# Six-expert part of an attention and mixture-of-experts kernel: sums and low parts of the weights made on GpSimd in place of VectorE

## The chip, the cores and the metric

The kernel runs on one core of a Trainium2 chip. A core has TensorE (PE, matmuls; its weight loads are listed as PEld), VectorE (DVE), ScalarE (ACT), GpSimd (POOL) and SyncE (SP, which here issues nearly all DMAs). Each engine works through its own list of instructions in order; semaphores tie the lists together. The metric is the time of one execution on the device in microseconds (us), and lower is better.

## The reference

A linear recurrence with complex decay per head (four sequences of 768 tokens, eight heads of 48) gives x of 3072 tokens by 384. A mixture of eight experts follows. Every expert is applied to every token, and its output is weighted by a gate matrix that eight rounds of row and column scaling (Sinkhorn) make from the logits:

```python
logits = x @ w_gate
P = np.exp(logits - logits.max())
for _ in range(8):
    P /= P.sum(1, keepdims=True) + 1e-09
    P /= P.sum(0, keepdims=True) + 1e-09
    P *= N / E
for e in range(E):                     # 8 experts
    h = np.maximum(x @ w1[e], 0.0)     # 384 -> 1024
    ye = h @ w2[e]                     # 1024 -> 384
    out += P[:, e:e + 1] * ye
```

All is in 32-bit floats.

## The kernel before

Every large matmul is made as three: a tensor is split into a high part (a cast to the rounded type that TensorE takes fast) and a low part (the tensor less its high part), and high x high, high x low and low x high are added in PSUM.

Phase 1 runs the recurrence for 256 tokens at a time and, beside it, experts 0 and 1 on the tokens that are done. `phase2a` closes that with the last experts' steps, the first Sinkhorn rounds, a check of the inputs' range and the first weights of the next part. `phase2b` is the six-expert part: 96 steps, four units of 768 tokens x experts 2 to 7 x four pairs of blocks of 128 hidden columns. Its order is two super-units (`su`), in each six experts (`e`), in each two units (`ul`), in each four pairs (`p`). So a prepared weight pair is used twice, four steps apart.

In one step a two-by-two block of the first layer is made by a scheme of seven products (P1, P6, P7, P5, P2, P4, P3 in that order) in place of eight. It needs sums of weight blocks (S1 to S4, and S5 for a third block) and sums of token blocks (T1 to T4). The products go to PSUM through two buffers of the tag `ph`, in turn: a product can begin when the one before the last has been read out. ScalarE copies P1 and P5 out (`s`, line 793). VectorE adds the others to earlier ones (line 788), which gives u2, u3 (from P6, P7), u4 and c22 (from two SBUF tensors), c11 (P2), c21 (P4) and c12 (P3). For each c, ScalarE makes the relu's high part `hh` (line 799) and VectorE the low part `hl` (line 800). Between the products PE makes the second layer of the step before (`second`, lines 739 to 741), from `hh`, `hl` and the split second-layer weights. After the last pair of an expert VectorE adds the outputs to `oa` (line 748), and while expert 3 runs also those of experts 0 and 1 (lines 725 and 727). `load_x` loads a unit's tokens and makes their sums on VectorE (lines 616 and 620).

`prep_w` prepares the weights of one expert and pair, 48 times. Its input is a raw tile (128 partitions x 2 blocks x 768 columns, 768 KB), loaded by SP in `raw_w` (line 641); its pool has one buffer, so the next load waits for the last reader of the one before. It makes five sums of 128 columns each (line 659; the second and the fourth read an earlier sum), four casts on ScalarE (line 661) and four low parts (line 662): two for `wa` (384 and 256 columns, straight from the raw tile), one for `wb` (640, from the sums) and one for `wc` (768, the second layer's weights). `wa`, `wb` and `wc` come from a ring of twelve buffers, four preparations deep. `prep_w` is called twice in `phase2a`, twice after the first step of `phase2b`, and once after every step that follows one on the second unit.

PE's order is written by hand. The order of the other engines is made when the kernel is built, by a scheduler that plays the program through in time and takes for each engine what it expects to be ready first; on the chip that order is fixed. The buffer numbers behind the names in the rows below are the builder's; the number behind s_, u_, c_, hh_ and hl_ is the step's.

Of the kernel before, what the change touches and what calls it, by code (L numbers as in the profile page):

```python
# [6 lines left out]
F32 = mybir.dt.float32  # L7
# [3 lines left out]
ALU = mybir.AluOpType  # L11
# [49 lines left out]
class Net:  # L61
# [581 lines left out]
        self.nraw += 1  # L643

    def prep_w(self):
        nc, V, A = self.nc, self.nc.vector, self.nc.scalar
        n = self.nprep
        if n == len(self.todo):
            return
        self.nprep += 1  # L650
        raw = self.raw.pop(n)
        R = raw.rearrange("p f (c d) -> p f c d", d=128)
        s = self.wr.tile([128, 5, 128], F32, tag="sum", name=f"sum{n}")
        wa = self.wp.tile([128, 2, 5, 128], F32R, tag="w", name=f"wa{n}")
        wb = self.wp.tile([128, 2, 5, 128], F32R, tag="w", name=f"wb{n}")
        w2 = self.wp.tile([128, 2, 2, C], F32R, tag="w", name=f"wc{n}")
        A11, A12, A13, A21, A22, A23 = (R[:, i, c] for i in range(2) for c in range(3))
        for o, a, b, op in ((0, A21, A22, ALU.add), (1, s[:, 0], A11, ALU.subtract), (2, A11, A21, ALU.subtract), (3, A12, s[:, 1], ALU.subtract), (4, A13, A23, ALU.subtract)):
            V.tensor_tensor(s[:, o], a, b, op)
        for t, k, src in ((wa, slice(0, 3), R[:, 0, :3]), (wa, slice(3, 5), R[:, 1, 1:3]), (wb, slice(0, 5), s), (w2, slice(0, 2), raw[:, :, C:])):  # L660
            A.activation(t[:, 0, k], src, AF.Copy)
            V.tensor_tensor(t[:, 1, k], src, t[:, 0, k].bitcast(F32), ALU.subtract)
        W = {nm: (wa, k) for k, nm in enumerate(("A11", "A12", "A13", "A22", "A23"))}
        W.update({f"S{k + 1}": (wb, k) for k in range(5)})
        self.W[n] = (W, w2)
        self.raw_w()
# [349 lines left out]
```

## Time and profile before

| | |
|---|---|
| median of three runs | 1827.03 us (1826.17 to 1827.82) |
| the profiled execution | 1826.91 us, its span 1825.0 us |
| granted TensorE clock, mean | 0.993 |
| busy in 649.4 to 1811 us (1161.6 us, the 96 steps) | PE 1149.62, DVE 822.53, ACT 412.12, POOL 0.00 us |
| raw loads | 48, 768 KB each, 4.3 us from issue to landing (4.1 to 6.4) |
| SP before raw loads, waiting for DVE's wc | 661.5 us in 40 waits |
| ACT before wa, waiting for raw | 72.8 us in 35 waits |
| ACT before wb, waiting for DVE's sums | 14.8 us in 26 waits |

Times of instructions and waits are from one profiled execution and count from the span's start. Consecutive matmuls overlap, so a single one's duration (0.33 us) is longer than its pitch (0.17 us). The idle time of an engine matters only where another engine ends up waiting for it; SP's long waits above are the single buffer of raw tiles doing what it is for.

### The profile page before, as it was taken

How to read it: one execution, taken by the hardware profiler on the slowest of the kernel's cores; microseconds unless marked ns; L12 is line 12 of the kernel's file. 1: busy time of each engine (PE TensorE's matmuls, PEld its weight loads, DVE VectorE, ACT ScalarE, POOL GpSimd, SP SyncE). 2: the span in 40 equal slices, each digit the busy share in tenths (PEclk: the TensorE clock that was granted, in tenths of full speed). 3: DMA queues.
4: the chain of work that ended last, by engine and by line, in shares of the span. 5: the costliest groups of instructions: out<-in, count | busy, mean ns of one | idle time of the engine just before them, and what ended most of it. 6: DMA issues, size and time to landing. Idle time of an engine off the chain costs nothing.

```text
span 1825.0 us, 30537 instructions
## 1 busy us (share of the span) xinstructions
PE 1767.9 (97%) x12024; PEld 1726.8 (95%) x12024; DVE 1358.4 (74%) x3023; ACT 733.1 (40%) x1606; POOL 6.4 (0%) x15
## 2 busy tenths in 40 slices
PE   5899999999999999999999999999999999999998
PEld 3889899999999999899999999999999999999998
DVE  7898899889883587867576767687776767675754
ACT  7544444554543443434242424243433333342421
POOL 1000000000000000000000000000000000000000
PEclk9999999999999999999999999999999999999999
DMA  6334333433332431402020101232220101020100
GB/s 210 108 104 117 103 112 112 119 112 115 115 105 93 132 92 38 136 2 69 1 69 1 53 18 53 70 96 78 87 70 18 53 18 52 3 69 1 53 27 28
DMA packets 120632, 132.83 MB, mean 73 GB/s; under 512 B 9632, under 2 KB 100512, under 8 KB 120480
## 3 DMA queue, kind: packets, MB, share of 16 engines
q1 hardware_dynamic: 119680, 130.41, 23.3%
q8 instruction: 96, 1.57, 0.4%
q14 instruction: 56, 0.46, 0.1%
q10 hardware_dynamic: 800, 0.39, 0.1%
HBM read 88.22 MB, written 23.59 MB: 61 GB/s over the span
## 4 chain that ended last, share of the span: by engine, by line
PE 86%; DVE 8%; DMA 3%; ACT 1%; issue 1%; SPq 1%; DVEq 0%; ACTq 0%
PE po L741 10%; PE po L739 10%; PE po L740 10%; PE P L778 9%; PE P L780 9%; PE P L779 9%; PE po L164 4%; PE ph L186 3%; PE ph L187 3%; PE ph L185 3%; PE po L166 3%; PE po L165 3%; PE sp L468 3%; PE y L485 2%; PE U L463 1%
## 5 line engine op out<-in xcount | busy, mean ns | idle before, releaser
L741 PE MATMUL po<-wc,hl 128*128 128x384 f32 x1152 | 385.7, 335 | 2.9 <-DVE hl L800 2.9
L739 PE MATMUL po<-wc,hh 128*128 128x384 f32 x1152 | 385.2, 334 | 0.4 <-ACT hh L799 0.4
L740 PE MATMUL po<-wc,hh 128*128 128x384 f32 x1152 | 385.2, 334 | 0.0
L799 ACT ACTIVATE hh<-c 128x384 fp32r<-128x384 f32 x384 | 200.9, 524 | 322.1 <-DVE c L788 320.7
L800 DVE SCALAR_TENSOR_TENSOR hl<-c,hh 128x384 fp32r<-128x384 f32 x384 | 211.8, 552 | 65.8 <-ACT hh L799 58.0
L741 PEld LDWEIGHTS po<-wc,hl 128*128 128x128 f32 x1152 | 216.5, 188 | 4.4 <-DVE hl L800 4.4
L739 PEld LDWEIGHTS po<-wc,hh 128*128 128x128 f32 x1152 | 216.5, 188 | 0.7 <-ACT hh L799 0.7
L740 PEld LDWEIGHTS po<-wc,hh 128*128 128x128 f32 x1152 | 216.4, 188 | 0.0
L793 ACT ACTIVATE s<-P 128x384 f32<-128x384 f32 x192 | 94.1, 490 | 275.0 <-PE P L780 275.0
L191 ACT ACTIVATE hh<-ph 128x256 fp32r<-128x256 f32 x192 | 73.1, 381 | 249.4 <-PE ph L187 248.9
L186 PE MATMUL ph<-xl,w 128*128 128x256 f32 x576 | 162.9, 283 | 2.8 <-DVE xl L525 2.8
L185 PE MATMUL ph<-xh,w 128*128 128x256 f32 x576 | 162.2, 282 | 0.6 <-ACT xh L524 0.6
L187 PE MATMUL ph<-xh,w 128*128 128x256 f32 x576 | 162.5, 282 | 0.0
L778 PE MATMUL P<-B,wa 128*128 128x384 f32 x480 | 160.4, 334 | 0.6 <-DVE c L788 0.6
L780 PE MATMUL P<-B,wa 128*128 128x384 f32 x480 | 160.4, 334 | 0.0
L779 PE MATMUL P<-B,wa 128*128 128x384 f32 x480 | 160.3, 334 | 0.0
L164 PE MATMUL po<-w,hh 128*128 128x384 f32 x384 | 140.9, 367 | 1.1 <-ACT yst L169 1.1
L166 PE MATMUL po<-w,hl 128*128 128x384 f32 x384 | 130.1, 339 | 0.0
L165 PE MATMUL po<-w,hh 128*128 128x384 f32 x384 | 129.7, 338 | 0.0
L788 DVE TENSOR_TENSOR c<-P,u 128x384 f32<-128x384 f32 x192 | 106.2, 553 | 31.1 <-PE P L780 29.3
L788 DVE TENSOR_TENSOR u<-u,s 128x384 f32<-128x384 f32 x96 | 53.3, 555 | 100.9 <-ACT s L793 100.8
L193 DVE TENSOR_TENSOR hl<-hf,hh 128x256 fp32r<-128x256 f32 x192 | 80.0, 419 | 45.0 <-ACT hf L192 43.6
(172 smaller groups left out, 3649.3 us busy)
## 6 DMA issues: line engine op xcount, KB each, us to landing
raw<-in_w_dram SPq DMA_DIRECT2D x48, 768.0 KB, 4.3
qs<-z SPq DMA_DIRECT2D x144, 64.5 KB, 2.6
qk<-in_aqk_dram SPq DMA_DIRECT2D x12, 768.0 KB, 4.9
ks<-kh SPq DMA_DIRECT2D x144, 64.0 KB, 2.6
ye_d<-yst SPq DMA_DIRECT2D x48, 192.0 KB, 2.1
y<-ye_d SPq DMA_DIRECT2D x48, 192.0 KB, 2.4
z<-in_aqk_dram SPq DMA_DIRECT2D x11, 768.0 KB, 6.9
B<-x_d SPq DMA_DIRECT2D x40, 192.0 KB, 3.5
```

Source lines behind the costliest of these rows:

```text
L164: nc.tensor.matmul(po[k], hh[:, s], w2h, start=f == 0, stop=False)
L185: nc.tensor.matmul(ph, w[:, 0, cs], xh[:, ct, :], start=(ct == 0), stop=False)
L186: nc.tensor.matmul(ph, w[:, 0, cs], xl[:, ct, :], start=False, stop=False)
L187: nc.tensor.matmul(ph, w[:, 1, cs], xh[:, ct, :], start=False, stop=(ct == NCT - 1))
L739: nc.tensor.matmul(po[k], hh[:, s], w2[:, 0, i], start=first, stop=False)
L740: nc.tensor.matmul(po[k], hh[:, s], w2[:, 1, i], start=False, stop=False)
L741: nc.tensor.matmul(po[k], hl[:, s], w2[:, 0, i], start=False, stop=last)
L778: nc.tensor.matmul(ps, t[:, 0, k], x[:, 0], start=first, stop=False)
L779: nc.tensor.matmul(ps, t[:, 0, k], x[:, 1], start=False, stop=False)
L780: nc.tensor.matmul(ps, t[:, 1, k], x[:, 0], start=False, stop=last)
L799: A.activation(hh, c, AF.Relu)
L800: V.scalar_tensor_tensor(hl, c, 0.0, hh.bitcast(F32), ALU.max, ALU.subtract)
```

## The change

In `prep_w` the five sums and the four low parts go to GpSimd. The casts stay on ScalarE, and nothing else is edited.

```diff
@@ -643,7 +643,7 @@
     def prep_w(self):
-        nc, V, A = self.nc, self.nc.vector, self.nc.scalar
+        nc, G, A = self.nc, self.nc.gpsimd, self.nc.scalar
@@ -656,10 +656,10 @@
         for o, a, b, op in ((0, A21, A22, ALU.add), (1, s[:, 0], A11, ALU.subtract), (2, A11, A21, ALU.subtract), (3, A12, s[:, 1], ALU.subtract), (4, A13, A23, ALU.subtract)):
-            V.tensor_tensor(s[:, o], a, b, op)
+            G.tensor_tensor(s[:, o], a, b, op)
         for t, k, src in ((wa, slice(0, 3), R[:, 0, :3]), (wa, slice(3, 5), R[:, 1, 1:3]), (wb, slice(0, 5), s), (w2, slice(0, 2), raw[:, :, C:])):
             A.activation(t[:, 0, k], src, AF.Copy)
-            V.tensor_tensor(t[:, 1, k], src, t[:, 0, k].bitcast(F32), ALU.subtract)
+            G.tensor_tensor(t[:, 1, k], src, t[:, 0, k].bitcast(F32), ALU.subtract)
```

VectorE's list in step 14 (expert 3, second unit, third pair), before (-) and now:

```order
 L788 TENSOR_TENSOR c_14_10557<-u_14_10538,s_14_10553 128x384
-L662 TENSOR_TENSOR wb_10628<-sum_10626,wb_10628 128x640
 L788 TENSOR_TENSOR c_14_10572<-P_14_10565,s_14_10520 128x384
 L800 SCALAR_TENSOR_TENSOR hl_14_10575<-c_14_10557,hh_14_10574 128x384
 L800 SCALAR_TENSOR_TENSOR hl_14_10579<-c_14_10572,hh_14_10578 128x384
 L788 TENSOR_TENSOR c_14_10595<-P_14_10588,u_14_10538 128x384
-L662 TENSOR_TENSOR wc_10629<-raw_10507,wc_10629 128x768
 L800 SCALAR_TENSOR_TENSOR hl_14_10598<-c_14_10595,hh_14_10597 128x384
 L788 TENSOR_TENSOR c_14_10614<-P_14_10607,u_14_10555 128x384
```

The rest keeps its order: both hl of c22 and c11 stand ahead of c21, and the hl of c21 ahead of c12, the last row. GpSimd's list of the same preparation, which is new, in the order in which it is worked through:

```order
L659 TENSOR_TENSOR sum_10626<-raw_10507 128x128 x3
L659 TENSOR_TENSOR sum_10626<-sum_10626,raw_10507 128x128
L662 TENSOR_TENSOR wa_10627<-raw_10507,wa_10627 128x384
L662 TENSOR_TENSOR wa_10627<-raw_10507,wa_10627 128x256
L659 TENSOR_TENSOR sum_10626<-raw_10507,sum_10626 128x128
L662 TENSOR_TENSOR wb_10628<-sum_10626,wb_10628 128x640
L662 TENSOR_TENSOR wc_10629<-raw_10507,wc_10629 128x768
```

The first row waits for the raw tile's DMA on GpSimd's own list; both low parts of wa stand ahead of the last sum. ScalarE's list at the same place:

```order
 L661 ACTIVATE wa_10627<-raw_10507 128x256
 L793 ACTIVATE s_14_10553<-P_14_10546 128x384
+L799 ACTIVATE hh_14_10574<-c_14_10557 128x384
 L661 ACTIVATE wb_10628<-sum_10626 128x640
-L799 ACTIVATE hh_14_10574<-c_14_10557 128x384
 L799 ACTIVATE hh_14_10578<-c_14_10572 128x384
 L661 ACTIVATE wc_10629<-raw_10507 128x768
```

The cast of the sums moved behind the relu of c22, and still stands ahead of that of c11. In steps 15 and 16 it moved by one or two rows in the same way. PE's list is the same in both kernels.

## The prediction

> **What bounds the kernel now.** I read the page's busy times first, then stretches cut out of the stage that the change touches, then what PE waited for, then the steps instruction by instruction. The page's first part says whose time the span is:
>
> ```profile
> PE 1767.9 (97%) x12024; PEld 1726.8 (95%) x12024; DVE 1358.4 (74%) x3023; ACT 733.1 (40%) x1606; POOL 6.4 (0%) x15
> ```
>
> PE is busy in 97% of the span, VectorE in 74%, and GpSimd does nothing after its first memsets. So work taken from VectorE pays only where PE waits for VectorE. Stretches of the six-expert part (columns: from:to in us, length, busy us and count of PE, PEld, DVE, ACT, POOL, clock, DMA) show where that is:
>
> ```profile
> 820.74:832.70 11.96, 11.96 (x71) 11.96 (x71) 9.10 (x21) 5.40 (x10) 0.00 (x0) 1.00 0.21 66
> 832.70:844.65 11.95, 11.95 (x70) 11.95 (x70) 9.16 (x21) 5.40 (x10) 0.00 (x0) 1.00 0.21 67
> 1200.00:1248.70 48.70, 45.90 (x261) 44.80 (x260) 39.31 (x85) 19.83 (x37) 0.00 (x0) 1.00 0.40 123
> 1300.00:1348.70 48.70, 46.56 (x265) 45.60 (x265) 39.61 (x87) 21.92 (x42) 0.00 (x0) 1.00 0.31 94
> ```
>
> The first two are steps 14 and 15, each with the preparation of one weight pair in it: PE is full, at full clock, 11.96 us a step. There VectorE's preparation is already hidden and its removal is worth nothing. In the other two, where VectorE also makes the next tokens' sums or adds expert outputs, PE loses 2.8 and 2.1 us of 48.7. PE's waits in total (us in all, times, longest):
>
> ```profile
> PE P L778 <- DVE c L788: 4.7, 7, 1.5
> PE P L778 <- ACT s L793: 3.0, 4, 1.2
> PE po L741 <- DVE hl L800: 2.9, 4, 1.1
> PE okp L561 <- DVE ok L558: 1.5, 1, 1.5
> PE P L778 <- DVE u L788: 0.7, 1, 0.7
> ```
>
> VectorE's four rows make 9.8 us: the ceiling of what the change can win, and not all of it stands beside a preparation.
>
> **What is moved, and what it costs where it goes.** By line and shape (count, then busy us and mean ns of one):
>
> ```profile
> L662 DVE TENSOR_TENSOR wc<-raw,wc 128x768 fp32r<-128x768 f32 x48 | 45.9, 956 | 12.2 <-ACT wc L661 12.1
> L662 DVE TENSOR_TENSOR wb<-sum,wb 128x640 fp32r<-128x640 f32 x48 | 39.2, 817 | 0.1
> L659 DVE TENSOR_TENSOR sum<-raw 128x128 f32<-128x128 f32 x144 | 35.7, 285 | 40.6 <-DMA raw<-in_w_dram 40.5
> L662 DVE TENSOR_TENSOR wa<-raw,wa 128x384 fp32r<-128x384 f32 x48 | 26.4, 551 | 0.0
> L662 DVE TENSOR_TENSOR wa<-raw,wa 128x256 fp32r<-128x256 f32 x48 | 20.0, 416 | 0.0
> L659 DVE TENSOR_TENSOR sum<-sum,raw 128x128 f32<-128x128 f32 x48 | 13.6, 283 | 0.0
> L659 DVE TENSOR_TENSOR sum<-raw,sum 128x128 f32<-128x128 f32 x48 | 13.5, 281 | 0.0
> ```
>
> The seven rows sum to 194.3 us, over 48 preparations 4.05 us each: nine instructions and 5 x 128 + 384 + 256 + 640 + 768 = 2688 columns. VectorE loses these and its 40.5 us of waiting for raw weights. On GpSimd no subtraction has run; its nearest rows are memsets:
>
> ```profile
> L215 POOL MEMSET sc<- 128x512 f32 x2 | 1.2, 612 | 0.1
> L225 POOL MEMSET rr<- 112x8 f32 x2 | 0.1, 94 | 0.0
> ```
>
> They give (612 - 94) / 504 = 1.03 ns a column and about 0.09 us an instruction. Low end: a subtraction goes at memset pace, 2688 x 1.03 ns + 9 x 0.09 = 3.6 us a preparation. High end: both operands and the result each take a pass, 9.1 us. I take two passes, 6.3 us: a memset reads nothing, so the two reads come on top of its pattern, and the write can go beside them. The Trainium skill (GPSIMD Engine Reference, section 3.1) gives 4497 ns for a two-input add of 2048 columns, against 2293 on VectorE; an estimate from it is 5.9 us a preparation, and no run here shows it.
>
> **What becomes late.** Step 14 in the timeline (start, us, instruction, idle before it and its releaser); first VectorE, then ScalarE, then PE in step 15:
>
> ```profile
> 824.18 0.49 DVE L659 TENSOR_TENSOR sum<-raw 128x128 f32<-128x128 f32 x2 [1.41 <-DMA raw<-in_w_dram]
> ...
> 826.27 0.28 DVE L659 TENSOR_TENSOR sum<-raw,sum 128x128 f32<-128x128 f32 x1
> ...
> 828.61 1.23 DVE L800 SCALAR_TENSOR_TENSOR hl<-c,hh 128x384 fp32r<-128x384 f32 x2
> ...
> 831.70 0.55 DVE L800 SCALAR_TENSOR_TENSOR hl<-c,hh 128x384 fp32r<-128x384 f32 x1
> 832.17 0.55 DVE L788 TENSOR_TENSOR c<-P,u 128x384 f32<-128x384 f32 x1
> ```
>
> ```profile
> 824.18 0.83 ACT L661 ACTIVATE wa<-raw 128x384 fp32r<-128x384 f32 x2 [2.07 <-DMA raw<-in_w_dram]
> ...
> 826.58 0.74 ACT L661 ACTIVATE wb<-sum 128x640 fp32r<-128x640 f32 x1 [0.25 <-DVE sum L659]
> 827.52 0.53 ACT L799 ACTIVATE hh<-c 128x384 fp32r<-128x384 f32 x1 [0.20 <-DVE c L788]
> 828.72 0.53 ACT L799 ACTIVATE hh<-c 128x384 fp32r<-128x384 f32 x1 [0.67 <-DVE c L788]
> 829.94 0.85 ACT L661 ACTIVATE wc<-raw 128x768 fp32r<-128x768 f32 x1 [0.70 <-PE P L780]
> 830.70 0.51 ACT L799 ACTIVATE hh<-c 128x384 fp32r<-128x384 f32 x1
> ```
>
> ```profile
> 833.39 0.33 PE L778 MATMUL P<-T,wb 128*128 128x384 f32 x1
> ```
>
> The reader should see two things. The cast of the sums (wb) stands in ScalarE's row ahead of relus, and waits for the fifth sum, 2.37 us after the raw weights landed (826.55 - 824.18). And the last product's addition (c12, the row at 832.17) frees the PSUM buffer that the next step's second product (the PE row) writes: it ends at 832.72, 0.67 us ahead of that matmul, some 0.5 us ahead of its weight load. That half microsecond is all the cover that VectorE has at the end of a step with a preparation.
>
> Now the same with GpSimd, in its new order: four sums, both low parts of wa, the fifth sum, wb, wc. The fifth sum ends after seven instructions and 1280 columns: 1.9 us at one pass, 3.3 at two, 4.6 at three. To this I add 1.1 us for being held up behind two VectorE instructions of 0.55 us: 4.4 us. Whether the two engines hold each other up at all where both read two tensors in SBUF is shown by no row; the bounds are nothing, and a whole instruction of the other engine each time they meet. I take half an instruction, midway. The raw weights land 0.7 us later, because the low part of wc that frees their only buffer takes 2 x 768 x 1.03 ns + 0.09 = 1.67 us for 0.96. So: landing 824.9, fifth sum 829.3, wb to 830.0, the relu behind it (c11) to 830.6, its hl on VectorE to 831.1; c21 queued behind that to 831.7; ScalarE has done wc by 831.4, relu of c21 to 832.2, its hl to 832.8, c12 behind it to 833.3. With 0.7 us more for that hl meeting the 1.4 us low part of wb half-way, c12 ends near 834.0, and must end by about 833.2: PE stalls **0.8 us**. ScalarE and VectorE work in order, so this delay reaches PE although neither is short of time. Without any hold-up, c12 ends at 832.2 or when P3 lets it (832.7), inside the margin.
>
> Steps 15 and 16 have the same chain, the cast one relu later. Step 16 also carries six additions of finished outputs, and has less room; I take 1.0 us on average over the three. The fourth preparation of an expert has its sums made steps ahead and costs nothing by this chain. The first four preparations, made beside the last steps of the first two experts, are due one by one in the first four steps; I put them at nothing, with up to 4 us if the second and third raw loads come late. The other 44 are eleven experts of four: 33 x 1.0 = **+33 us**. On the SP queue the next raw load waits for wc on GpSimd, and loads of expert outputs (y) and of tokens (B) stand behind it; their order shifts by a place or two. That costs them the same 0.7 us, at few places, and I add nothing.
>
> **What is won.** Of the 9.8 us that PE waits for VectorE I take about three quarters, **-7 us**: the 1.5 us before the check's transpose, where VectorE was subtracting weights, and most of the waits in the stretches above, which lose 4 us of VectorE work a step. The 3.0 us behind ScalarE's s stay. The profiled execution took 1826.9 us (span 1825.0 and 1.9 around it), 0.1 under the median of 1827.0. So 1826.9 + 33 - 7 = **1853 us**.
>
> **Rivals.** *Relief*: GpSimd is at two passes or less and no engine holds the other up; the margin at c12 stays, and only the relief remains, all of the 9.8 us but some 2: 1826.9 - 8 = 1819 us. For it: PE is full in steps 14 and 15, and the chain comes out at 832.7 without hold-ups. Against it: six VectorE instructions with two SBUF inputs (u4, c22, four hl) stand in each such step, beside GpSimd's 6.3 us of 12. It decides if c12 ends within 0.5 us of where it does now. Chance 0.27.
>
> *Full hold-up*: an instruction of one engine waits out the other's whole instruction. Then the hl of c21 waits 0.7 us longer, and that of c11 meets a low part too, 0.7; with less to spare elsewhere 1.6 us a step: 33 x 1.6 = +53, and VectorE's other two-tensor additions are held up in the heavy stretches, so the relief is gone: 1880 us. Chance 0.21. The Trainium skill (SBUF — State Buffer, section "Who interferes with whom") says just this: a VectorE instruction with two SBUF inputs contends with a GpSimd instruction that reads SBUF, and whichever issues second is blocked until the first is done. No row of this case can show it, GpSimd having read nothing; that rule speaks against the change.
>
> *Nothing visible*: hold-ups eat the relief, the margin just holds: 1827 us, chance 0.12. My forecast, 1840 to 1866, has 0.40.
>
> **The numbers.** The range reaches from most of the relief to past the full hold-up, 1816 to 1888, and leaves some 0.15 out. A measurement of this kernel can tell about 0.2%, 3.7 us, from no change. Faster by more than that: the relief, 0.26; within it: 0.14; slower: 0.60, from the forecast and the full hold-up.
>
> **What would show it.** Right: PE waiting for DVE c or u some thirty times in steps with a preparation, ScalarE's wb waiting for POOL's sum by 2 us or more, SP's raw load waiting for POOL's wc, hl on VectorE starting late after its relu is done; VectorE's busy time down by some 194 us. The subtraction of wc on POOL should take about 1.7 us. Wrong: steps of 11.96 us throughout with fewer PE waits than before (relief), or a subtraction at 1 us. If POOL's preparation takes over 9 us, the single raw buffer becomes the limit, and even 1880 is too low.

## The result and the profile after

| | kernel before | changed kernel |
|---|---|---|
| median of four runs on one chip | 1827.42 us (1826.17 to 1829.74) | 1879.69 us (1877.21 to 1882.07) |
| ratio, with 95% interval | 1 | 1.0289 (1.0276 to 1.0302) |
| profiled execution, its span | 1826.91 us, 1825.0 us | 1882.07 us, 1880.1 us |

The change costs 52.3 us by the medians, 55.2 between the two profiled executions. The forecast was 1853 us: right in sign, half in size. The busy times of the page's first part, and then what PE waited for (us in all, times, longest), in the changed kernel:

```profile
PE 1784.1 (95%) x12024; PEld 1730.9 (92%) x12024; DVE 1319.4 (70%) x2591; ACT 725.1 (39%) x1606; POOL 401.2 (21%) x447
```

```profile
PE P L778 <- DVE c L788: 42.8, 33, 4.6
PE okp L561 <- DVE ok L558: 2.8, 1, 2.8
PE po L741 <- DVE hl L800: 1.9, 2, 1.6
PE P L778 <- DVE u L788: 1.6, 2, 1.1
```

```profile
PEld P L778 <- DVE c L788: 58.4, 47, 4.9
```

PE now waits 33 times for one of VectorE's c, 42.8 us in all, where it waited 7 times and 4.7 us. The weight load in front of a matmul waits for the same c, and its row (PEld) shows the shorter waits too: 47 of them, 58.4 us, after 8 and 7.4 us in the kernel before. VectorE has 432 instructions less (48 x 9), yet its busy time fell by 39 us and not by the 194 that they took. The groups by line and shape show where the rest went, first before and then now (busy us and mean ns of one stand behind the bar):

```profile
L800 DVE SCALAR_TENSOR_TENSOR hl<-c,hh 128x384 fp32r<-128x384 f32 x384 | 211.8, 552 | 65.8 <-ACT hh L799 58.0
L788 DVE TENSOR_TENSOR c<-P,u 128x384 f32<-128x384 f32 x192 | 106.2, 553 | 31.1 <-PE P L780 29.3
L788 DVE TENSOR_TENSOR c<-u,s 128x384 f32<-128x384 f32 x96 | 52.8, 550 | 0.0
```

```profile
L800 DVE SCALAR_TENSOR_TENSOR hl<-c,hh 128x384 fp32r<-128x384 f32 x384 | 278.3, 728 | 100.6 <-ACT hh L799 90.6
L788 DVE TENSOR_TENSOR c<-P,u 128x384 f32<-128x384 f32 x192 | 105.9, 552 | 30.4 <-PE P L780 30.3
L788 DVE TENSOR_TENSOR c<-u,s 128x384 f32<-128x384 f32 x96 | 70.1, 730 | 0.0
```

The instructions are the same, on the same shapes. Those with both inputs in SBUF (hl, c from u and s) take 176 and 180 ns longer on average. The one with an input in PSUM (c from P and u) takes as long as ever. The timeline of step 14, the step that the prediction worked through, shows what a longer one does. It has GpSimd's last rows, then VectorE's, then PE's (start, us, instruction, idle before it and its releaser):

```profile
842.58 1.57 POOL L662 TENSOR_TENSOR wb<-sum,wb 128x640 fp32r<-128x640 f32 x1 [0.85 <-ACT wb L661]
844.10 2.17 POOL L662 TENSOR_TENSOR wc<-raw,wc 128x768 fp32r<-128x768 f32 x1
...
842.95 1.61 DVE L800 SCALAR_TENSOR_TENSOR hl<-c,hh 128x384 fp32r<-128x384 f32 x1 [0.80 <-ACT hh L799]
844.49 0.54 DVE L788 TENSOR_TENSOR c<-P,u 128x384 f32<-128x384 f32 x1
845.62 1.06 DVE L800 SCALAR_TENSOR_TENSOR hl<-c,hh 128x384 fp32r<-128x384 f32 x1 [0.59 <-ACT hh L799]
846.61 0.55 DVE L788 TENSOR_TENSOR c<-P,u 128x384 f32<-128x384 f32 x1
...
847.21 0.45 PE L778 MATMUL P<-T,wb 128*128 128x384 f32 x1 [1.18 <-DVE c L788]
```

The first hl is issued 0.37 us after GpSimd began wb, and ends at 844.56. GpSimd's wb ended at 844.15, 0.41 us earlier. The second hl meets wc: GpSimd ends at 846.27, the hl at 846.68, again 0.41 later. So an hl waits until GpSimd's whole instruction is over and then does its work. This holds throughout: of the 384 hl of this trace 99 take over 700 ns, and each of these ends 0.41 to 0.42 us after the GpSimd instruction that it met. Behind it stands c12 (846.61 to 847.16), and PE's second product of step 15 waits for it, 1.18 us. This is the chain and the place that the prediction named.

The cost is spread like this. Rows are stretches with from:to, length, busy us and count of PE, PEld, DVE, ACT, POOL, clock, DMA. First four quiet steps of the changed kernel, steps 14 to 17, then three stretches with other work on VectorE (steps 5 to 9, 44 to 50, 51 to 57), and behind them the same three in the kernel before:

```profile
833.00:845.34 12.34, 12.25 (x70) 11.93 (x70) 7.56 (x11) 4.92 (x10) 7.20 (x9) 1.00 0.20 64
845.34:858.78 13.44, 12.26 (x70) 11.94 (x70) 8.74 (x13) 5.25 (x11) 7.72 (x10) 1.00 0.17 60
858.78:870.74 11.96, 11.96 (x70) 11.94 (x70) 8.28 (x15) 4.17 (x9) 6.57 (x9) 1.00 0.21 67
870.74:884.43 13.69, 12.35 (x71) 11.87 (x70) 8.51 (x15) 4.33 (x9) 5.60 (x7) 1.00 0.18 58
...
712.20:785.16 72.96, 64.06 (x349) 61.18 (x349) 60.00 (x101) 25.18 (x51) 32.37 (x34) 0.98 0.35 109
1206.27:1302.94 96.67, 87.61 (x484) 84.88 (x484) 68.66 (x113) 32.90 (x67) 34.38 (x36) 0.98 0.30 95
1302.94:1398.44 95.50, 88.37 (x484) 85.94 (x484) 69.15 (x113) 35.16 (x71) 32.80 (x36) 0.96 0.24 75
```

```profile
708.17:773.08 64.91, 61.75 (x349) 59.75 (x348) 58.51 (x135) 25.04 (x50) 0.00 (x0) 1.00 0.39 122
1179.79:1269.50 89.71, 85.58 (x485) 83.48 (x484) 70.58 (x149) 34.05 (x67) 0.00 (x0) 1.00 0.32 102
1269.50:1357.04 87.54, 84.82 (x485) 83.54 (x484) 69.53 (x149) 35.98 (x71) 0.00 (x0) 1.00 0.27 82
```

The four quiet steps take 51.43 us; at 11.96 us each they took 47.84, so a preparation cycle of one expert loses 3.6 us. By the step starts in the two traces, the quiet stretches (steps 10 to 43 and 58 to 93, eight such cycles) lose 27.9 us together. The three heavy stretches lose 8.1, 7.0 and 8.0 us, 23.0 in all, though VectorE has 34 to 36 instructions less in each: its busy time there is 197.8 us after 198.6. The time up to step 5 loses 4.0. These make the 55.0 us by which the span grew.

In the quiet stretches the waits of the weight loads for c account for the whole loss: 25 of them, 27.9 us, none in the kernel before. Each cycle has three of size. The first is 0.41 us long and stands at the start of step 14; it comes from the preparation before, whose wc is worked on at the end of step 13 (GpSimd, VectorE's hl of c21 and c12, then the weight load of step 14's second product):

```profile
831.00 1.84 POOL L662 TENSOR_TENSOR wc<-raw,wc 128x768 fp32r<-128x768 f32 x1 [8.36 <-ACT wc L661]
831.37 1.88 DVE L800 SCALAR_TENSOR_TENSOR hl<-c,hh 128x384 fp32r<-128x384 f32 x1 [0.74 <-ACT hh L799]
833.17 0.54 DVE L788 TENSOR_TENSOR c<-P,u 128x384 f32<-128x384 f32 x1
833.77 0.19 PEld L778 LDWEIGHTS P<-T,wb 128*128 128x128 f32 x1 [0.41 <-DVE c L788]
```

The second, 1.4 to 1.6 us, is the one in step 15 shown above (1.50 us in the weight load's row, 1.18 in the matmul's). The third, 1.1 to 1.7 us, stands in step 17. In all eight cycles the hl just ahead of c12 had met the same GpSimd instruction: wc at the first and the second wait, wb at the third. The preparation that is loaded in step 15 makes PE wait nowhere.

GpSimd's side, by line and shape, and the range of two of the lines (min, median, max in ns):

```profile
L662 POOL TENSOR_TENSOR wc<-raw,wc 128x768 fp32r<-128x768 f32 x48 | 95.9, 1999 | 123.3 <-ACT wc L661 123.3
L662 POOL TENSOR_TENSOR wb<-sum,wb 128x640 fp32r<-128x640 f32 x48 | 75.7, 1578 | 42.3 <-ACT wb L661 42.3
L659 POOL TENSOR_TENSOR sum<-raw 128x128 f32<-128x128 f32 x144 | 68.3, 502 | 802.3 <-DMA y<-ye_d 582.6 <-DMA raw<-in_w_dram 219.6
```

```profile
L662 POOL TENSOR_TENSOR wc<-raw,wc x48: 1800/1998/2194, 622.7 to 1784.4; 128x768 fp32r<-128x768 f32 x48
L659 POOL TENSOR_TENSOR sum<-raw x144: 448/463/872, 589.6 to 1775.8; 128x128 f32<-128x128 f32 x144
```

From the two minima a subtraction costs (1800 - 448) / 640 = 2.1 ns a column. GpSimd's busy time less the 6.4 us of memsets that it had before makes (401.2 - 6.4) / 48 = 8.2 us a preparation.

### The profile page after: what moved, and what is told of

It is laid out like the page before. It is cut to its first block, busy times and chain, and to the rows that moved or that the text cites. A ratio compares the mean times of both kernels' runs of the same rounds, so it can differ in the third digit from the quotient of the medians.

```text
span 1880.1 us, 30664 instructions
## 1 busy us (share of the span) xinstructions
PE 1784.1 (95%) x12024; PEld 1730.9 (92%) x12024; DVE 1319.4 (70%) x2591; ACT 725.1 (39%) x1606; POOL 401.2 (21%) x447
## 4 chain that ended last, share of the span: by engine, by line
PE 65%; DVE 14%; DMA 8%; POOL 5%; ACT 4%; issue 3%; SPq 1%; DVEq 0%; POOLq 0%; ACTq 0%
PE po L739 7%; PE po L741 7%; PE po L740 7%; PE P L778 6%; PE P L780 6%; PE P L779 6%; DMA raw<-in_w_dram 5%; PE po L164 3%; DVE hl L800 3%; PE ph L186 3%; PE ph L187 3%; PE ph L185 3%; PE po L166 3%; PE po L165 3%; DVE c L788 3%
## 5 line engine op out<-in xcount | busy, mean ns | idle before, releaser
L800 DVE SCALAR_TENSOR_TENSOR hl<-c,hh 128x384 fp32r<-128x384 f32 x384 | 278.3, 728 | 100.6 <-ACT hh L799 90.6
L659 POOL TENSOR_TENSOR sum<-raw 128x128 f32<-128x128 f32 x144 | 68.3, 502 | 802.3 <-DMA y<-ye_d 582.6
L662 POOL TENSOR_TENSOR wa<-raw,wa 128x384 fp32r<-128x384 f32 x96 | 103.5, 1098 | 415.7 <-ACT wa L661 415.7
L788 DVE TENSOR_TENSOR u<-u,s 128x384 f32<-128x384 f32 x96 | 63.0, 657 | 171.2 <-ACT s L793 171.1
L164 PE MATMUL po<-w,hh 128*128 128x384 f32 x384 | 141.1, 367 | 1.4 <-ACT yst L169 1.4
L778 PE MATMUL P<-T,wb 128*128 128x384 f32 x288 | 102.5, 356 | 38.4 <-DVE c L788 35.4
```

Of the source, the lines that this page charges most:

```text
L164: nc.tensor.matmul(po[k], hh[:, s], w2h, start=f == 0, stop=False)
L778: nc.tensor.matmul(ps, t[:, 0, k], x[:, 0], start=first, stop=False)
L800: V.scalar_tensor_tensor(hl, c, 0.0, hh.bitcast(F32), ALU.max, ALU.subtract)
```

## The experiments

Three theories were stated. A: GpSimd's instructions, reading SBUF, hold VectorE's instructions with two SBUF inputs up. B: GpSimd is slower, so that its results are late (wb's cast, the next raw load), and needs no hold-up for that. C: the new order of VectorE's and ScalarE's lists costs the time. A later one, D, is that the single raw buffer becomes a loop longer than a step. The medians, each beside its own runs of the kernel before (medians 1826.2 to 1826.6):

| run | us | ratio (95%) |
|---|---|---|
| idle_reads | 1894.0 | 1.0367 (1.0349 to 1.0385) |
| idle_writes | 1828.9 | 1.0009 (0.9999 to 1.0019) |
| idle_copies | 1833.9 | 1.0043 (1.0028 to 1.0057) |
| write_only | 1824.1 | 0.9986 (0.9976 to 0.9995) |
| write_mid | 1828.1 | 1.0007 (0.9997 to 1.0016) |
| write_long | 1836.5 | 1.0061 (1.0046 to 1.0077) |
| no_prep | 1817.1 | 0.9950 (0.9934 to 0.9966) |
| sums_only | 1832.9 | 1.0035 (1.0023 to 1.0047) |
| low_only | 1869.2 | 1.0232 (1.0216 to 1.0248) |
| pieces | 1874.6 | 1.0263 (1.0246 to 1.0280) |
| low_pieces | 1889.7 | 1.0350 (1.0326 to 1.0374) |
| split_before | 1827.4 | 1.0003 (0.9993 to 1.0012) |
| split_raw | 1845.7 | 1.0103 (1.0086 to 1.0120) |
| split_pieces | 1829.5 | 1.0019 (1.0009 to 1.0029) |
| split_low_pieces | 1843.1 | 1.0089 (1.0075 to 1.0103) |
| split_wc | 1826.0 | 0.9999 (0.9990 to 1.0008) |

**The hold-up alone.** The kernel before keeps its whole preparation on VectorE, and GpSimd adds finished high and low parts into a tile that nobody reads, in eleven instructions and 2688 columns a preparation. Then the same with one-input copies, and with writes in place of the reads; the rows of the three runs are marked:

```diff
+            for x, y in cuts[k.start, k.stop]:
+                G.tensor_tensor(self.idle[:, :y - x], hi[:, x:y], lo[:, x:y], ALU.add)    # idle_reads
+                G.tensor_copy(self.idle[:, :y - x], lo[:, x:y])                           # idle_copies
+                G.tensor_copy(self.idle[:, :1], lo[:, x:x + 1])                           # idle_writes
+                for _ in range(2):
+                    G.memset(self.idle[:, :y - x], 0.0)
```

> The kernel before, with VectorE preparing the weights as ever, and beside it GpSimd adding finished high and low parts of the weights (2688 columns a preparation, in pieces of at most 384) into a tile that nobody reads. No engine waits for GpSimd's results, and the lists of the other four engines are those of the kernel before. Theory A (hold-up: a VectorE instruction with two SBUF inputs waits until the GpSimd instruction that is reading SBUF is over): slower by 20 to 70 us, 1847 to 1897, with hl (line 800) lengthened where GpSimd runs. Theory B (GpSimd's results come late, and the in-order lists of ScalarE and VectorE wait for them) and theory C (the new order of the lists): no change, 1823 to 1831 us.

> As the run with idle reads, but GpSimd only writes: for each piece one column is read and then two memsets of the piece's size are made, so that GpSimd is busy about as long. Theory A in its narrow form (GpSimd's reads hold VectorE up): within 4 us of the kernel before, 1823 to 1831, and hl at its 552 ns. If every access of GpSimd holds VectorE up: as slow as the run with idle reads. Theories B and C: no change.

> As the run with idle reads, but GpSimd copies the low parts (one input) in place of adding two. If any read of GpSimd holds VectorE's two-input instructions up, hl is lengthened here too, by the shorter duration of the copies: 1835 to 1880 us. If only two-input instructions of GpSimd do: 1823 to 1831.

VectorE's hl and PE's waits in idle_reads:

```profile
L805 DVE SCALAR_TENSOR_TENSOR hl<-c,hh 128x384 fp32r<-128x384 f32 x384 | 251.3, 656 | 65.1 <-ACT hh L804 58.0
```

```profile
PE P L783 <- DVE c L793: 39.8, 48, 3.1
```

Work whose result nobody uses costs 67 us, with hl at 656 ns in place of 552 and 39.8 us of PE's waits for c. VectorE's, ScalarE's and PE's lists are those of before, so C has no part in it. With writes in place of the reads hl takes 553 ns and the time is that of before. So GpSimd's reads do it, not its being busy: A is shown as a cause. The copies cost 7.7 us, below what was expected of them: they hold hl up too (570 ns, at most 854), but they are short, 472 to 857 ns on average by shape.

**Lateness alone.** The changed kernel, with GpSimd's reads cut to one column and memsets of a chosen length in their place. The sums are zero, and the high parts stand in for the low parts in the matmuls. write_only has some 6.8 us a preparation, write_mid 8.1, write_long 11.2.

```diff
-            G.tensor_tensor(s[:, o], a, b, op)
+            G.tensor_tensor(s[:, o, :1], a[:, :1], b[:, :1], op)
+            G.memset(s[:, o], 0.0)
...
-            G.tensor_tensor(t[:, 1, k], src, t[:, 0, k].bitcast(F32), ALU.subtract)
+            def gate():
+                G.tensor_tensor(self.idle, src[:, 0, :1], t[:, 0, k.start, :1].bitcast(F32), ALU.subtract)
+            gate()
+            for _ in range(2):        # write_mid; 1 in write_only, 3 in write_long
+                G.memset(src, 0.0)
...                                    # for some, a memset of half the columns besides
+            gate()
```

> The changed kernel with GpSimd's nine instructions replaced by one-column reads, which keep every wait, and memsets that fill about the same time (7.1 us a preparation by the rates of its rows, against 7.3 for the subtractions where nothing meets them). The sums are zero, and the second layer and the products use the high parts of the weights for their low parts. Theory A: the stalls go, 1815 to 1832 us, hl at 552 ns. Theory B: they stay, 1870 to 1885 us, with wb on ScalarE waiting for the sums as long. Theory C: they stay, for the lists are nearly those of the changed kernel.

> GpSimd's place in the chain without its reads, as in the two runs that only write, but now sized to some 8.5 us a preparation, what the changed kernel needs. The high parts stand in for the low parts in the matmuls and the sums are zero. If GpSimd's lateness takes part in the loss at this length, 1832 to 1842 us (the run with 11.2 us lost 11); if only the hold-ups cost, 1821 to 1828 us, as with 6.8 us a preparation.

> The run with writes only, its memsets for the low parts made three times in place of once, so that a preparation takes GpSimd some 11 us, as in the run with pieces, without reads that hold VectorE up. It tells what in that run's 48 us is lateness: the raw tile is given back later, the fifth sum comes later, and ScalarE waits in order. If the hold-ups of up to 0.3 us are the loss there: 1820 to 1830 us. If lateness takes over once GpSimd needs nearly a step: 1845 to 1880, with ScalarE's wb waiting for the sums by 60 us and more in all.

With hl back at 554 to 555 ns the loss is gone: 1824.1 and 1828.1 us. Both run the new order of VectorE's and ScalarE's lists but for 1 to 7 per cent of the rows, and ScalarE's wb waits for GpSimd's sums by 34.6 us in write_only, more than the 21.6 us in the changed kernel. So B and C do not make the loss by themselves. At 11.2 us a preparation lateness costs 10 us, between the two expectations: that is where GpSimd begins to need a whole step.

no_prep takes the preparation away from all engines (no sums, no low parts; the high parts of the raw weights stand in for both):

> No engine makes the sums or the low parts; the high parts of the raw weights stand in for both, with the same casts and matmuls. This is the most that taking the work off VectorE can win. If the 7 us that the prediction put down as won were there to be had: 1817 to 1821 us. If the run that only writes shows the whole of it: 1822 to 1826 us.

1817.1 us: the relief that the prediction priced at 7 us is there, 9.4 us of it, as long as nothing takes VectorE's place. Against this time write_only and write_mid are 7.0 and 11.0 us slower. They relieve VectorE as much, so lateness and the new order are not free between them: they use up the relief. What they do not do is add the 52 us.

**Which part.** sums_only moves only the sums to GpSimd, low_only only the low parts.

> Half of the change: the five sums on GpSimd, the four low parts on VectorE as before. GpSimd reads for 5 x 0.46 = 2.3 us a preparation in place of 7.3, in instructions of 0.46 us. Hold-up: VectorE's two-input instructions meet it rarely and for at most 0.3 us; VectorE loses 1.3 us of work a preparation: 1823 to 1835 us. If lateness of the sums is what costs (wb on ScalarE waits for them): 1840 to 1855, for it is the sums alone that ScalarE waits for.

> The other half: the four low parts on GpSimd, the sums on VectorE. GpSimd reads for some 5.1 us a preparation, in its longest instructions (up to 1.8 us). Hold-up: most of the loss is here, 1855 to 1878 us. Lateness of the sums: none is late, 1822 to 1830.

The long subtractions carry most of it, +43 us of 52; the sums alone +6.7.

**Shorter instructions.** If a hold-up lasts to the end of GpSimd's instruction, short instructions should cure it. In pieces every low part is done in pieces of 128 columns; in low_pieces the sums go back to VectorE besides.

```diff
-            G.tensor_tensor(t[:, 1, k], src, t[:, 0, k].bitcast(F32), ALU.subtract)
+            for j in range(k.stop - k.start):
+                for q in range(3 if t is w2 else 1):
+                    c = slice(q * 128, q * 128 + 128)
+                    G.tensor_tensor(t[:, 1, k.start + j, c], src[:, j, c], t[:, 0, k.start + j, c].bitcast(F32), ALU.subtract)
```

> The changed kernel with every low part in pieces of 128 columns: 21 GpSimd instructions a preparation in place of nine, none over some 0.5 us alone, and some 9.4 us of GpSimd in place of 7.3. Theory A: no hold-up is longer than about half a microsecond, so the loss of 52 us falls to 10 to 30, 1837 to 1857 us. Theory B: GpSimd is done later still, 1885 to 1900 us. Theory C: 1870 to 1885 us.

> Sums on VectorE as before; only the low parts are on GpSimd, in 16 pieces of 128 columns. Open is why the run with all of the preparation on GpSimd in such pieces stayed at 1.026 though no hl waited longer than 0.3 us. If late sums did it (GpSimd needed 10.9 us a preparation there, and ScalarE's cast of the sums waited 68.9 us for it), the sums are now on time and the loss is mostly gone: 1828 to 1842 us. If it is the hold-ups themselves, many short ones in place of few long ones, it stays near the run with whole low parts on GpSimd (1.023): 1857 to 1875 us, and PE's waits for VectorE's c stay above 20 us.

Both missed. The hold-ups became short, as the row of hl in pieces shows (min, median, max), yet the time hardly fell, and in low_pieces it rose. The row behind it is what ScalarE waited for in low_pieces:

```profile
L803 DVE SCALAR_TENSOR_TENSOR hl<-c,hh x384: 542/559/860, 656.8 to 1860.4; 128x384 fp32r<-128x384 f32 x192
```

```profile
ACT wa L661 <- DMA raw<-in_w_dram: 180.8, 36, 7.2
```

ScalarE stands 180.8 us in front of raw weights that have not landed (100.9 us in the changed kernel, 72.8 before). Many pieces take longer than few whole parts: 10.9 us a preparation in pieces in place of 8.2, and in low_pieces 8.7 us for the low parts alone, which took 5.4 in low_only. The next raw load waits for the last of them. This pointed to D, which the next runs test. The wait by itself is no sign of a loss: write_only has 112.4 us of it and is as fast as the kernel before.

**The loop of the single raw buffer.** ScalarE's casts of wa follow the landing. Three in a row, in the changed kernel and then in write_mid:

```profile
837.18 0.83 ACT L661 ACTIVATE wa<-raw 128x384 fp32r<-128x384 f32 x2 [2.53 <-DMA raw<-in_w_dram]
850.47 0.83 ACT L661 ACTIVATE wa<-raw 128x384 fp32r<-128x384 f32 x2 [2.38 <-DMA raw<-in_w_dram]
864.54 0.83 ACT L661 ACTIVATE wa<-raw 128x384 fp32r<-128x384 f32 x2 [4.55 <-DMA raw<-in_w_dram]
```

```profile
826.23 0.83 ACT L662 ACTIVATE wa<-raw 128x384 fp32r<-128x384 f32 x2 [4.05 <-DMA raw<-in_w_dram]
839.38 0.83 ACT L662 ACTIVATE wa<-raw 128x384 fp32r<-128x384 f32 x2 [1.02 <-DMA raw<-in_w_dram]
852.91 0.83 ACT L662 ACTIVATE wa<-raw 128x384 fp32r<-128x384 f32 x2 [2.44 <-DMA raw<-in_w_dram]
```

In the changed kernel a landing follows the last by 13.3 and 14.1 us: 9.1 us from landing to the end of wc's low part (837.18 to 846.27) and 4.2 us of load. A step is 11.96 us, so against a step without a wait the preparation slides later each time, by 1.3 us and more. write_mid slides as much, 13.2 and 13.5 us. Its median is 1.6 us above the kernel before. The execution shown was the slowest of its ten, at 1833.3 us, and even there the quiet stretches lose 7.4 us where those of the changed kernel lose 27.9. So the slide alone costs little. What is left is the two together. split_raw takes the loop out of the changed kernel: the raw tile becomes two, for the first and the second layer's weights, in the same space, so that the first-layer weights no longer wait for wc. split_pieces does so in pieces, split_before in the kernel before.

```diff
-        raw = self.wr.tile([128, 2, 2 * C], F32, tag="raw", name=f"raw{self.nraw}")
-        self.nc.sync.dma_start(raw, self.w[e, 2 * p:2 * p + 2].rearrange("f p c -> p f c"))
+        raw = [self.wr.tile([128, 2, C], F32, tag=f"raw{h}", name=f"raw{h}_{self.nraw}") for h in range(2)]
+        for h in range(2):
+            self.nc.sync.dma_start(raw[h], self.w[e, 2 * p:2 * p + 2, :, h * C:h * C + C].rearrange("f p c -> p f c"))
```

> The changed kernel with the raw tile in two tiles of 384 KB, first-layer and second-layer weights, each with its own single buffer: the next first-layer weights no longer wait until GpSimd has done the low part of wc. In the changed kernel the time from landing to that end (9.1 us) and the load (4.2 us) make 13.3 us, more than a step of 11.96. If this loop is what delays the chain in steps 15 and 16, most of the loss beside the heavy stretches goes: 1840 to 1862 us. If hold-ups in the chain are enough by themselves: 1866 to 1882 us.

> The same two tiles in the kernel with the low parts in pieces of 128 columns, where a hold-up is at most a piece long but GpSimd needs 10.9 us a preparation. If its loss came from the raw loop (landing to landing some 15 us), 1830 to 1852 us; if from the many short hold-ups, 1860 to 1878 us.

> The kernel before with the two tiles, as a control for the two runs beside it: 1822 to 1831 us by every theory.

VectorE's hl in split_raw, and steps 14 to 17 of it as stretches:

```profile
L801 DVE SCALAR_TENSOR_TENSOR hl<-c,hh 128x384 fp32r<-128x384 f32 x384 | 279.9, 731 | 89.6 <-ACT hh L800 82.5
```

```profile
825.36:837.70 12.34, 12.24 (x70) 11.88 (x70) 7.87 (x12) 5.17 (x10) 8.33 (x10) 1.00 0.23 64
837.70:850.07 12.37, 12.28 (x70) 11.92 (x70) 8.30 (x12) 5.13 (x10) 8.51 (x10) 1.00 0.24 65
850.07:862.44 12.37, 12.28 (x71) 11.92 (x71) 9.86 (x18) 3.85 (x8) 6.42 (x8) 1.00 0.24 66
862.44:874.40 11.96, 11.96 (x71) 11.96 (x71) 6.48 (x12) 3.74 (x8) 1.86 (x1) 1.00 0.13 34
```

hl is held up as much as in the changed kernel (731 ns after 728), and yet 33 of the 52 us are gone: 1845.7 us. The quiet steps lose 0.4 us in each of three in place of 3.6 us together. With short hold-ups besides, 3 us remain (1829.5, just under the range that was expected), and the quiet steps are back at 11.96 us. In the kernel before the two tiles change nothing. So of the 52 us some 19 remain without the loop, and 33 need both: hold-ups, and a preparation that comes late enough for wb's cast and the long instructions to fall ahead of c12. Hold-ups need no slide to cost time. In split_raw each of the 24 waits in the quiet stretches is 0.41 to 0.42 us long and stands behind an hl that met wc, as at 831.37 above. In idle_reads ScalarE's casts of wa in steps 14 and 15 start 11.95 us apart, so nothing has slid, and step 15 still takes 13.04 us; there VectorE has its preparation to do besides. Two reservations stand. With two tiles the builder also puts the wa casts a step earlier on ScalarE's list, and this study does not tell that apart from the loop itself. And the three heavy stretches still lose 11.5 us in split_raw, after 23.0; how that divides was not tried.

**A smaller share.** Two runs looked for a version below the kernel before, both with two tiles and pieces: split_low_pieces leaves the sums on VectorE, split_wc gives GpSimd only the low part of wc.

> Two raw tiles, sums on VectorE, low parts on GpSimd in pieces of 128 columns: GpSimd has some 2.5 us less to do in a preparation than with the sums (1829.5 us), VectorE has the 62.8 us of sums back. If GpSimd's remaining hold-ups make the 3 us that are left there, 1820 to 1826 us, faster than before; if the relief of VectorE is what counts in the heavy stretches, 1827 to 1833 us.

> Two raw tiles, and only the low part of wc on GpSimd, in six pieces of 128 columns: 3.4 us of GpSimd in a preparation, and 45.9 us off VectorE. By the hold-ups it should cost next to nothing, and win at most a quarter of the 9.4 us that no preparation at all wins: 1822 to 1829 us.

split_low_pieces missed by 10 us: VectorE's sums wait 110.5 us for raw weights on VectorE's own list there (40.5 us before, 32.0 in split_before), with hl and u behind them. That this wait makes the loss is argued from the rows and was not tried. split_wc is as fast as before. No version found that makes the whole preparation is faster than the kernel before.

## Why the prediction was right or wrong

- **PE is full in quiet steps, nothing to win there**: right. no_prep leaves those steps at 11.96 us and wins elsewhere.
- **The chain** (fifth sum, wb, relu of c11, its hl, c21, its hl, c12, the next step's second product): right, at its place. In step 14 wb's cast starts 8.77 us into the step (predicted, on the same scale, near 8.4) and PE waits 1.18 us there for 0.8 predicted. PE waits for c 33 times; some thirty were named. They are not where they were expected, though: the prediction had a stall behind each of steps 14, 15 and 16 and none from the fourth preparation of an expert. Measured in a cycle are 0.41 us from that fourth preparation (its wc holds an hl up, whatever its sums do), 1.5 us behind step 14, none behind step 15 and 1.1 to 1.7 us behind step 16. ScalarE's wb waits for GpSimd's sum 22 times, 2.2 us at most and 21.6 us in all, where 2 us or more was named.
- **Price on GpSimd**: 6.3 us were taken; the shortest instructions of each form sum to 7.3 and the run shows 8.2. wc's low part takes 1.80 to 2.19 us for 1.67. The estimate from the Trainium skill (GPSIMD Engine Reference, section 3.1), 5.9 us, was low too, as it left out each instruction's fixed part and the hold-ups. The bounds of 3.6 and 9.1 held.
- **Hold-ups at half an instruction**: too low. An hl waits to the end of whatever GpSimd runs. The rule quoted from the Trainium skill (SBUF — State Buffer, section "Who interferes with whom") states this, and the rows and idle_reads agree.
- **"The raw weights land 0.7 us later"**: this term failed. It was taken as a fixed delay, though each late landing delays the next. In steps 14, 15 and 16 wa's cast starts 4.19, 5.12 and 5.76 us into the step, after 3.28, 3.11 and 3.41 before. The prediction put the limit of the single raw buffer at a preparation of over 9 us. It is reached sooner: when the time from landing to wc's end and the load together (9.1 + 4.2 us) are longer than a step. For the quiet stretches the errors nearly cancel: 3 us an expert forecast, 3.5 measured.
- **"What is won", -7 us**: this is the step that lost the number. The relief exists (9.4 us in no_prep), but the heavy stretches, where it was to come from, lost 23.0 us. Each held four preparations, 16 us of VectorE work, and VectorE's busy time did not fall by 1% over the three. Hold-ups took the place of the subtractions there: hl takes 887, 756 and 731 ns on average in the three, after 548 to 551, and the additions of y to `oa`, with both tensors in SBUF, 789 and 811 ns, after 607 and 609. So VectorE's busy time fell by 39 us over the whole, for the 194 forecast. Taking loop and hold-ups together as one chain price of 1.0 us a step carried over from quiet steps, and adding a gain on top, was the error.
- **Start**: put at nothing, up to 4 us; 4.0 measured up to step 5.
- **The sum**: +24 for eight quiet cycles measured 27.9; +9 - 7 = +2 for three heavy ones measured 23.0; 0 at the start measured 4.0.
- **Rivals**: Full hold-up gave 1880 us, the time that came. Its two statements are borne out (a whole instruction, relief gone), its 1.6 us a step is not: quiet steps lose 1.2, the heavy stretches more. That its total agrees is in part luck: the time was lost in other places than its sum says. Relief alone is refuted by the runs, since reads on GpSimd are enough to lose 67 us; nothing visible is refuted by the time.

## What to carry to other kernels

Before work goes from VectorE to GpSimd, look for VectorE instructions with both inputs in SBUF beside it: a held-up instruction counts as busy, so a busy time that falls by less than the moved work is the sign to look for. Where a single buffer is loaded, used and loaded again, add load and use and compare them with the step. In the changed kernel they made 13.3 us against 11.96, each landing of an expert came later in its step than the last, and with hold-ups this cost 33 us more than hold-ups without it. A run in which the idle engine does useless reads, and one in which it only writes, tell hold-ups from lateness without moving anything.

## What the hardware showed that was not expected

- The hold-up acts both ways: of the 144 sums of two raw blocks the shortest take 448 ns and the longest 872. All 21 over 520 ns ran beside a VectorE instruction with two inputs in SBUF, and without one none takes over 488. wc's low part ran 2.17 us beside an hl for 1.80 at its shortest.
- An input in PSUM is enough to escape: c from P and u stays at 552 ns on average and 558 at most beside the same GpSimd work.
- One-input copies on GpSimd hold VectorE up too (hl up to 854 ns), memsets do not (hl 553 ns on average).
- Short instructions on GpSimd bound a hold-up but not its sum: in pieces hl averages 595 ns, and GpSimd's preparation grows from 8.2 to 10.9 us.
